# P.V of the first seven units in column tiles, with one Ln and one product for both heads

## The chip, the cores and the metric

The kernel runs on one core of one Trainium2 chip. The metric is device time in microseconds (us). A ratio is the mean time of one kernel's fast runs over that of the kernel before's fast runs in the same rounds, on the same chip, so it is not quite the ratio of the medians that are quoted beside it. The engines are TensorE (PE), ScalarE (ACT), VectorE (DVE), GpSimd (POOL, which issues most transfers here) and SyncE (SP).

## The reference

Attention with a relative position bias, then a layer with a squared ReLU. Cut to what matters:

```python
batch, n_heads, seq, head_dim = (8, 8, 576, 64)
scores = scale * np.matmul(q, k.transpose(0, 1, 3, 2)) + bias          # bias by distance, 32 buckets
attn = np.exp(scores - max)
attn = attn / (np.sum(attn, axis=-1, keepdims=True) + 1e-09)
x = np.matmul(attn, v)                                                  # "P.V"
h = np.maximum(x @ w_in, 0.0)                                           # 512 -> 2048
out = h * h @ w_out                                                     # 2048 -> 512
```

## The kernel before

A *unit* is two heads and 192 queries; there are 96. For each, TensorE makes the scores, ScalarE the exponentials, VectorE multiplies in the bias. P.V then gives the values and, from a column block of constants beside V, the sums. The weights of one head's key tile are 128 columns: 64 of V and 64 of constants. So one head takes one PSUM bank, values in one half of the partitions and sums in the other (the second head the other way round), and five matmuls:

```python
def pv_mm(e, jts):                       # e: which head of the two
    def f():
        if (n, e) not in pvt:
            pv_tile(n, e)                # one bank a head
        for jt in jts:                   # key tiles; jt 4 is the shared short one
            pv = pvt[n, e][:, 0:IC]      # 128 partitions x 192
            io(nc.tensor.matmul(
                pv if jt < 4 else pv.rearrange("p (g c) -> p g c", g=2),
                vz[:, jt, 2 * hp + e, :],                                  # 128 columns
                ets[n, jt // 2][:, e, ds(jt % 2 * IC, IC)] if jt < 4 else last_keys(n),
                start=(not mixed and jt == 0), stop=(jt == 3)))
```

The division is done as values x exp(-ln(sums)): one Ln a head, one Exp for both, one product a head:

```python
def ln(e):                                       # ScalarE, out of the sums' half of the bank
    ...
    nc.scalar.activation(out=rs[n][o : o + 64, :], in_=pvt[n, e][64 - o : 128 - o, 0:IC], func=LNF)
...
def mult(e):                                     # VectorE; a bank is free after its product
    ...
    nc.vector.tensor_tensor(out=x_sb[o : o + 64, hp, ds(ring(blk), IC)][:, ::-1],
                            in0=pvt[n, e][o : o + 64, 0:IC], in1=rs[n][o : o + 64, :], op=MULT)
```

The order on each engine is not written by hand. Every operation is recorded with estimated durations and its dependencies, and a list scheduler puts all of them in order when the kernel is built. One estimate: 0.095 us on TensorE when the row tiling changes. From unit 17 on another form of P.V is used, which this change does not touch.

The softmax here doesn't subtract the row's maximum and nothing guards it: scores larger than these inputs give would overflow.

Of the kernel before, what the change touches and what calls it, by code (L numbers as in the profile page):

```python
# [12 lines left out]
FP32 = mybir.dt.float32  # L13
FP16 = mybir.dt.float16
EXPF = mybir.ActivationFunctionType.Exp
LNF = mybir.ActivationFunctionType.Ln
RELUF = mybir.ActivationFunctionType.Relu
COPYF = mybir.ActivationFunctionType.Copy
MULT = mybir.AluOpType.mult
# [5 lines left out]
IC, NB = 192, 3  # L25
# [9 lines left out]
P, T0 = 4.07, 8.0  # L35


PV_BANKS, PV_MORE = [("p0", "p1"), ("f1", "f2")], 7


F1_LAG, F2_LAG = 4.8, 19.5
# [50 lines left out]
class Plan:  # L92
# [10 lines left out]
    def add(self, eng, stream, occ, lat, fn, deps=(), due=0.0, load=0.0, rows=128, more=False):  # L103
        o = Op(eng, occ, lat, fn, deps, due, load, rows, more)
        self.streams.setdefault(eng, {}).setdefault(stream, deque()).append(o)
        return o
# [78 lines left out]
def kernel(  # L185
# [10 lines left out]
    nc = tc.nc  # L196
    assert (_bucket(np.arange(128, S)) == NBK - 1).all()

    def io(ins):
        return tc.keep_in_program_order(ins)  # L200
# [15 lines left out]
    nr_pool = ctx.enter_context(tc.tile_pool(name="nr", bufs=2))  # L216
# [20 lines left out]
    x_sb = single.tile([128, 4, RING], FP16, name="x_sb")  # L237
# [9 lines left out]
    add = plan.add  # L247
# [81 lines left out]
    for out_, in_, t in (  # L329
# [9 lines left out]
            name=nc.get_next_instruction_name(),  # L339
# [123 lines left out]
    qts, kts, sts, ets, rs, pvt, hpt, rts, ypt, yts, tpt = ({} for _ in range(11))  # L463
# [3 lines left out]
    banks = {"f1": None, "f2": None, "p0": tv, "p1": warmed, "s0": None, "s1": None}  # L467
# [2 lines left out]
    plan.wait = lambda: 0.3 if units[0] < RUN_FROM else 0.02  # L470
    plan.fill = (lambda: units[0] == 0, 0.12, lambda: warm_up(1))
    s_last, kq_ready = {}, {}
    mults, ets_last, pv_ops = {}, {}, {}
    block_mults, f1_ops, f2_ops, sq_ops = {}, {}, {}, {}

    first_use = {4 * b + hp: n for n, (b, ic, hp) in reversed(list(enumerate(UNITS)))}
# [226 lines left out]
    def last_keys(n, rows=slice(None)):  # L703

        return ets[n, 0][rows, :, 2 * IC :]

    def values_need(n, e, jts=range(5)):

        b, ic, hp = UNITS[n]
        loads = [x for h_, x in zip([0, 0, 1, 1, 2, 3, 4, 5, 6, 7], loads_v[b]) if h_ in (e, 2 * hp + e)]  # L710
        return [o for g in {jt // 2 % 2 for jt in jts} for o in ets_last[n, g]] + loads

    def values_banks(o, n, es):


        def need(at):
            best = None
            for tags in [vbank[n]] if n in vbank else PV_BANKS if n < PV_MORE else PV_BANKS[:1]:
                x = [banks[tags[e]] for e in es]
                if not any(i.at is None for i in x if i):  # L720
                    t = max([at] + [i.done for i in x if i])
                    if best is None or t < best[0]:
                        best = t, tags
            return best

        def took(tags):
            vbank[n] = tags
            for e in es:
                banks[tags[e]] = mults[n][e]
            units[0] = n + 1  # L730

        o.need, o.took = need, took

    def pv_tile(n, e):
        tag = vbank[n][e]
        pvt[n, e] = (psF if tag[0] == "f" else psP).tile([128, 512], FP32, tag=tag, name=f"pv{e}")
        return pvt[n, e]
# [23 lines left out]
    def values(n, mixed=None):  # L761

        b, ic, hp = UNITS[n]
        vz = vzs[b % 2]
        pieces = ((0, 1), (2, 3)) if mixed else ((0, 1, 4), (2, 3))

        def pv_mm(e, jts):
            def f():
                if (n, e) not in pvt:
                    pv_tile(n, e)  # L770
                for jt in jts:
                    pv = pvt[n, e][:, 0:IC]
                    io(
                        nc.tensor.matmul(  # L774
                            pv if jt < 4 else pv.rearrange("p (g c) -> p g c", g=2),
                            vz[:, jt, 2 * hp + e, :],
                            ets[n, jt // 2][:, e, ds(jt % 2 * IC, IC)] if jt < 4 else last_keys(n),
                            start=(not mixed and jt == 0),
                            stop=(jt == 3),
                        )  # L780
                    )

            return f

        pv_ops[n] = []
        for e in range(2):
            for jts in pieces:
                o = add(
                    "PE",
                    "pv",  # L790
                    0.0825 * len(jts),
                    0.0825 * len(jts) + 0.22,
                    pv_mm(e, jts),
                    values_need(n, e, jts) + [mixed],
                    T0 + P * (n + 1.1 + 0.1 * e if mixed else n + 1.6 + 0.1 * e),
                )
                if not mixed and jts[0] == 0:
                    values_banks(o, n, (e,))
            pv_ops[n].append(o)

    def ring(blk):
        return blk * IC % RING

    def normalise(n):

        b, ic, hp = UNITS[n]
        blk = NB * b + ic
        mults[n] = []

        def ln(e):  # L810
            def f():
                if e == 0:
                    rs[n] = nr_pool.tile([128, IC], FP32, tag="r", name="r")
                o = 64 * e
                io(
                    nc.scalar.activation(  # L816
                        out=rs[n][o : o + 64, :], in_=pvt[n, e][64 - o : 128 - o, 0:IC], func=LNF
                    )
                )

            return f

        def mult(e):
            def f():
                o = 64 * e
                io(
                    nc.vector.tensor_tensor(  # L827
                        out=x_sb[o : o + 64, hp, ds(ring(blk), IC)][:, ::-1],
                        in0=pvt[n, e][o : o + 64, 0:IC],
                        in1=rs[n][o : o + 64, :],  # L830
                        op=MULT,
                    )
                )

            return f

        lns = [
            add("ACT", "ln", 0.31, 0.38, ln(e), [pv_ops[n][e]] + (mults[n - 2] if n > 1 else []), T0 + P * (n + 1.3))
            for e in range(2)
        ]  # L840
        x = add(
            "ACT",
            "ln",
            0.26,
            0.41,
            lambda: io(nc.scalar.activation(out=rs[n], in_=rs[n], func=EXPF, scale=-1.0)),  # L846
            lns,
            T0 + P * (n + 1.3),
        )
        free = f1_ops.get(blk - RING // IC, [])  # L850
        for e in range(2):
            mults[n].append(add("DVE", "mult", 0.29, 0.42, mult(e), [x] + free, T0 + P * (n + 1)))
        block_mults.setdefault(blk, []).extend(mults[n])


# [176 lines left out]
    for n in range(N + 1):  # L1032
        if RUN_FROM < n < N:
            mixed_in = []
            scores(n, lambda *x: mixed_in.append(values_mixed(n - 1, *x)))
            values(n - 1, *mixed_in)
        else:
            if n < N:
                scores(n)
            if n:  # L1040
                values(n - 1)
        if n:
            normalise(n - 1)
            for blks in GROUPS:
                if n - 1 == max(i for i, (b, ic, hp) in enumerate(UNITS) if NB * b + ic in blks):
                    layer1(blks)
                    layer2(blks)
        if n == N:
            break
        b, ic, hp = UNITS[n]  # L1050
        if last_use[4 * b + hp] == n:
            keys(4 * b + hp + KB)
        if b and (ic, hp) == (0, 0) and b < B - 1:

            loads_v[b + 1] = [x for i in range(8) for x in load_v(b + 1, i, pv_ops[n - 1])]
        if b and (ic, hp) == (1, 0) and b + 2 < B:
            halves[b + 2] = halve(b + 2)
# [32 lines left out]
```

## Time and profile before

| | before |
|---|---|
| time | 426.37 us, median of 3 (426.30 to 426.77); with later runs of the same build 426.34 |
| span of the profiled run | 422.2 us |
| busy, share of the span | PE 96%, DVE 74%, ACT 72% |

The span of a profile is some 1.8 us shorter than the time of the same run. In the first sixth the three engines wait for each other, so that is where fewer or shorter ScalarE and VectorE instructions can pay. The lines that show this, and what TensorE does later, stand in the prediction.

### The profile page before, as it was taken

The page shows a single profiled execution, that of the slowest core. Times are in us where ns is not written, and L with a number is a line of the kernel's source. Part 1 is how long each engine was busy: PE and PEld are TensorE (multiplying, and loading weights), DVE is VectorE, ACT ScalarE, POOL GpSimd, SP SyncE. Part 2 cuts the span into 40 slices and gives each one's busy share as a digit, 9 for nine tenths or more (in the row PEclk, how much of TensorE's full clock was granted, in tenths as well). Part 3 has the DMA queues.
Part 4 walks back from the last instruction along what each step waited for, and adds up shares of the span by engine and source line. Part 5 has one row for each costly group of instructions (what it writes and reads, how often), then busy time and mean ns, then how long its engine had stood idle before and what let it go on. Part 6 is the DMA issues. An engine that isn't in the chain of part 4 may idle for free.

```text
span 422.2 us, 9448 instructions
## 1 busy us (share of the span) xinstructions
PE 406.7 (96%) x3631; PEld 262.0 (62%) x3631; DVE 313.5 (74%) x940; ACT 302.9 (72%) x588; POOL 130.7 (31%) x176
## 2 busy tenths in 40 slices
PE   7888989899999999999999999999999999999996
PEld 4666876466685666666666566666666666665554
DVE  6889687668785777777776878777777877778762
ACT  5898796797897887787778777887787777770000
POOL 7956649409400491008600391006000000000000
PEclk8899999999999999999999999999999999999999
DMA  9999999969965699159925599169004110001012
GB/s 136 152 200 149 176 135 77 149 119 83 123 66 99 92 102 93 54 103 92 127 35 87 96 100 105 47 92 107 26 22 69 49 50 2 26 26 51 25 51 75
DMA packets 164765, 36.61 MB, mean 87 GB/s; under 512 B 152584, under 2 KB 160064, under 8 KB 164720
## 3 DMA queue, kind: packets, MB, share of 16 engines
q0 software_dynamic: 129728, 19.11, 59.1%
q1 hardware_dynamic: 34896, 16.90, 16.4%
q8 instruction: 28, 0.46, 0.5%
q14 instruction: 17, 0.14, 0.1%
q10 hardware_dynamic: 96, 0.00, 0.0%
HBM read 37.56 MB, written 16.52 MB: 128 GB/s over the span
## 4 chain that ended last, share of the span: by engine, by line
PE 85%; DVE 9%; ACT 3%; issue 1%; DMA 1%; DVEq 0%
PE yps L985 29%; PE hps L902 27%; PE pv L774 15%; PE st L640 7%; PE pv L748 3%; PE st L615 2%; DVE y L998 2%; DVE et L684 2%; ACT et L666 2%; DVE x_sb L827 1%; DVE rt L921 1%; DVE g_sb L917 1%; DMA raw_k<-in_k_dram 1%; PE tp L502 1%; ACT r L816 1%
## 5 line engine op out<-in xcount | busy, mean ns | idle before, releaser
L666 ACT ACTIVATE et<-st 128x960 f16<-128x960 f32 x192 | 167.9, 883 | 55.0 <-PE st L640 54.1
L902 PE MATMUL hps<-x_sb,w_in_sb 128*128 128x384 f16 (+1 forms) x896 | 152.0, 303 | 1.1 <-DVE rt L921 0.6
L985 PE MATMUL yps<-w_out_sb,g_sb 128*128 128x512 f16 (+1 forms) x592 | 148.6, 373 | 2.6 <-DVE y L998 1.7
L902 PEld LDWEIGHTS <-w_in_sb 128*128 128x128 f16 x896 | 83.3, 98 | 49.8 <-issue 2.1
L684 DVE TENSOR_TENSOR et<-et,tb_sb 128x384 f16<-128x384 f16 (+2 forms) x288 | 78.2, 310 | 33.3 <-ACT et L666 29.6
L251 POOL DMA_DIRECT2D vz<-in_v_dram x80 | 57.8, 743 | 129.4 <-PE pv L774 72.6
L985 PEld LDWEIGHTS <-g_sb 128*128 128x128 f16 x592 | 57.2, 98 | 51.1 <-issue 6.0
L774 PE MATMUL pv<-et,vz 128*128 128x192 f16 x804 | 84.9, 247 | 2.8 <-DVE x_sb L827 1.6
L827 DVE TENSOR_TENSOR x_sb<-pv,r 64x192 f16<-64x192 f32 x192 | 67.8, 353 | 21.6 <-ACT r L846 18.3
L917 DVE TENSOR_TENSOR g_sb<-rt 128x384 f16<-128x384 f16 x192 | 68.0, 358 | 7.5 <-ACT rt L913 2.5
L774 PEld LDWEIGHTS <-vz 128*128 128x128 f16 x804 | 62.4, 98 | 18.0 <-issue 15.2
L816 ACT ACTIVATE r<-pv 64x192 f32<-64x192 f32 x192 | 62.6, 326 | 7.7 <-PE pv L774 2.8
L913 ACT ACTIVATE rt<-hps 128x384 f16<-128x384 f32 x96 | 46.7, 487 | 28.6 <-PE hps L902 28.4
L921 DVE TENSOR_SCALAR rt<-hps 128x384 f16<-128x384 f32 x96 | 53.5, 557 | 13.4 <-PE hps L902 10.3
L640 PE MATMUL st<-qt,kt 64*128 64x192 f16 x768 | 50.2, 246 | 0.6 <-ACT et L666 0.6
L251 POOL DMA_DIRECT2D k<-in_k_dram x48 | 31.0, 684 | 27.4 <-DMA q<-in_q_dram 16.2
L846 ACT ACTIVATE r<-r 128x192 f32<-128x192 f32 x96 | 35.0, 364 | 3.1
L640 PEld LDWEIGHTS <-kt 64*128 64x128 f16 x768 | 31.9, 95 | 3.5 <-issue 1.5
L998 DVE TENSOR_SCALAR y<-yps 128x512 f32<-128x512 f32 (+1 forms) x37 | 25.0, 676 | 7.6 <-PE yps L985 6.8
L615 PEld LDWEIGHTS <-km_sb 128*128 128x128 f16 x192 | 18.2, 99 | 17.4 <-issue 3.0
L615 PE MATMUL st<-qt,km_sb 128*128 128x96 f16 x192 | 24.2, 208 | 0.7 <-ACT et L666 0.5
L251 POOL DMA_DIRECT2D q<-in_q_dram x18 | 24.6, 1401 | 0.0
(33 smaller groups left out, 117.1 us busy)
## 6 DMA issues: line engine op xcount, KB each, us to landing
out_dram<-y SPq DMA_DIRECT2D x35, 256.0 KB, 2.5
vz<-in_v_dram POOLq DMA_DIRECT2D x64, 64.0 KB, 3.1
q<-in_q_dram POOLq DMA_DIRECT2D x18, 192.0 KB, 8.2
k<-in_k_dram POOLq DMA_DIRECT2D x48, 72.0 KB, 7.0
w_in_sb<-in_moe_w_in_dram POOLq DMA_DIRECT2D x4, 512.0 KB, 9.5
w_out_sb<-in_moe_w_out_dram POOLq DMA_DIRECT2D x4, 512.0 KB, 9.8
qh<-in_q_dram POOLq DMA_DIRECT2D x8, 144.0 KB, 6.4
kh<-in_k_dram POOLq DMA_DIRECT2D x7, 144.0 KB, 7.2
```

Source lines behind the costliest of these rows:

```text
L251: return lambda: io(eng.dma_start(out=out_, in_=in_))
L615: nc.tensor.matmul(st[:, g, 2 * IC : 2 * IC + IC // 2], km_sb[:, p % KB, :], qts[p][:, ds(c0 + g * IC // 2, IC // 2)], start=True, stop=True,)
L640: nc.tensor.matmul(st[:, e, ds(i * IC, IC)], kts[p][rows, ts(2 * g + i, 128)], qts[p][rows, ds(c0, IC)], start=True, stop=True,)
L666: io(nc.scalar.activation(out=et, in_=sts[n, g][:, :, 0:w], func=EXPF, scale=SCALE))
L684: nc.vector.tensor_tensor(out=sl, in0=sl, in1=tb_sb[:, 2 * hp : 2 * hp + 2, ds(w0, w)], op=MULT)
L774: nc.tensor.matmul(pv if jt < 4 else pv.rearrange("p (g c) -> p g c", g=2), vz[:, jt, 2 * hp + e, :], ets[n, jt // 2][:, e, ds(jt % 2 * IC ...
L816: nc.scalar.activation(out=rs[n][o : o + 64, :], in_=pvt[n, e][64 - o : 128 - o, 0:IC], func=LNF)
L827: nc.vector.tensor_tensor(out=x_sb[o : o + 64, hp, ds(ring(blk), IC)][:, ::-1], in0=pvt[n, e][o : o + 64, 0:IC], in1=rs[n][o : o + 64, :], ...
L902: nc.tensor.matmul(hps[:, ds(i * w, w)], w_in_sb[:, kk, ts(nt, 128)], x_sb[:, kk, ds(o, w)], start=(kk == 0), stop=(kk == 3),)
L917: io(nc.vector.tensor_tensor(out=g_sb[:, ts(u, k), o : o + w], in0=rt, in1=rt, op=MULT))
L921: io(nc.vector.tensor_scalar_max(out=rt, in0=hpt[blks, u][:, 0 : 2 * IC], scalar1=0.0))
L985: nc.tensor.matmul(ypt[j], g_sb[:, nt, ds(128 * m % RING, 128)], w_out_sb[:, nt, cols], start=(nt == 0), stop=(nt == 15),)
```

## The change

Its intent: put the values of both heads into one bank and the sums of both into another. Each 128-column matmul then becomes two of 64 columns; the two heads' matmuls go to different column halves of the array, where they can run at the same time. One Ln over 128 partitions then serves both heads, and so does one product. Only the first seven units get this form (`COLS`).

```diff
+COLS = 7
...
+        def columns(jts):
+            def f():
...
+                for jt in jts:
+                    for u in range(2):           # 0: values, 1: sums; one bank each
+                        for e in range(2):       # head e in partitions 64 e and up
+                            pv = pvt[n, u][64 * e : 64 * e + 64, 0:IC]
+                            io(nc.tensor.matmul(
...
+                                    vz[:, jt, 2 * hp + e, ds(64 * (u ^ e), 64)],
...
+        def ln_both():
+            io(nc.scalar.activation(out=rs[n], in_=pvt[n, 1][:, 0:IC], func=LNF))
+
+        def mult_both():
+            io(nc.vector.tensor_tensor(
+                    out=x_sb[:, hp, ds(ring(blk), IC)][:, ::-1], in0=pvt[n, 0][:, 0:IC], in1=rs[n], op=MULT))
...
-                banks[tags[e]] = mults[n][e]
+                banks[tags[e]] = mults[n][e] if n >= COLS or e == 0 else lns[n]
```

The cuts leave out the recording of these operations with the scheduler (P.V of a unit in two pieces of 12 and 8 matmuls, Ln and product of 0.31 and 0.29 us) and line breaks.

More of the change, by code (lines that the diff above doesn't have):

```diff
@@ L472 @@
     s_last, kq_ready = {}, {}
-    mults, ets_last, pv_ops = {}, {}, {}
+    mults, lns, ets_last, pv_ops = {}, {}, {}, {}
     block_mults, f1_ops, f2_ops, sq_ops = {}, {}, {}, {}
@@ L785, in values @@
         pv_ops[n] = []
+        def columns(jts):
+            def f():
+                if (n, 0) not in pvt:
+                    for u in range(2):
+                        pv_tile(n, u)
+                for jt in jts:
+                    for u in range(2):
+                        for e in range(2):
+                            pv = pvt[n, u][64 * e : 64 * e + 64, 0:IC]
+                            io(
+                                nc.tensor.matmul(
+                                    pv if jt < 4 else pv.rearrange("p (g c) -> p g c", g=2),
+                                    vz[:, jt, 2 * hp + e, ds(64 * (u ^ e), 64)],
+                                    ets[n, jt // 2][:, e, ds(jt % 2 * IC, IC)] if jt < 4 else last_keys(n),
+                                    start=(jt == 0),
+                                    stop=(jt == 3),
+                                )
+                            )
+            return f
+        if n < COLS:
+            for jts in pieces:
+                o = add(
+                    "PE",
+                    "pv",
+                    0.165 * len(jts) + 0.1,
+                    0.165 * len(jts) + 0.32,
+                    columns(jts),
+                    values_need(n, 0, jts) + values_need(n, 1, jts),
+                    T0 + P * (n + 1.6),
+                )
+                if jts[0] == 0:
+                    values_banks(o, n, (0, 1))
+            pv_ops[n].append(o)
+            return
         for e in range(2):
@@ L808, in normalise @@
         mults[n] = []
+        def ln_both():
+            rs[n] = nr_pool.tile([128, IC], FP32, tag="r", name="r")
+            io(nc.scalar.activation(out=rs[n], in_=pvt[n, 1][:, 0:IC], func=LNF))
+        def mult_both():
+            io(
+                nc.vector.tensor_tensor(
+                    out=x_sb[:, hp, ds(ring(blk), IC)][:, ::-1], in0=pvt[n, 0][:, 0:IC], in1=rs[n], op=MULT
+                )
+            )
         def ln(e):
@@ L835, in mult @@
             return f
-        lns = [
-            add("ACT", "ln", 0.31, 0.38, ln(e), [pv_ops[n][e]] + (mults[n - 2] if n > 1 else []), T0 + P * (n + 1.3))
-            for e in range(2)
-        ]
+        war = mults[n - 2] if n > 1 else []
+        if n < COLS:
+            x = [lns.setdefault(n, add("ACT", "ln", 0.31, 0.38, ln_both, pv_ops[n] + war, T0 + P * (n + 1.3)))]
+        else:
+            x = [
+                add("ACT", "ln", 0.31, 0.38, ln(e), [pv_ops[n][e]] + war, T0 + P * (n + 1.3)) for e in range(2)
+            ]
         x = add(
@@ L846, in normalise @@
             lambda: io(nc.scalar.activation(out=rs[n], in_=rs[n], func=EXPF, scale=-1.0)),
-            lns,
+            x,
             T0 + P * (n + 1.3),
@@ L850, in normalise @@
         free = f1_ops.get(blk - RING // IC, [])
-        for e in range(2):
-            mults[n].append(add("DVE", "mult", 0.29, 0.42, mult(e), [x] + free, T0 + P * (n + 1)))
+        for f in [mult_both] if n < COLS else [mult(e) for e in range(2)]:
+            mults[n].append(add("DVE", "mult", 0.29, 0.42, f, [x] + free, T0 + P * (n + 1)))
         block_mults.setdefault(blk, []).extend(mults[n])
```

## The prediction

> **What bounds the kernel now.** I read the page first, then windows, then the chain and the timeline of the part that the change touches. Columns of the windows view: stretch, its length, then busy us of PE, PE's weight load, DVE, ACT and POOL with instruction counts, clock, DMA share, GB/s.
>
> ```profile
> span 422.2 us, 9448 instructions
> PE 406.7 (96%) x3631; PEld 262.0 (62%) x3631; DVE 313.5 (74%) x940; ACT 302.9 (72%) x588; POOL 130.7 (31%) x176
> ...
> PE   7888989899999999999999999999999999999996
> ```
>
> Each digit is a tenth of busy time in one fortieth (10.6 us) of the span. From about 60 us on TensorE (PE) is full, so there the end moves by PE's own work alone. The first sixth is different, and all seven units of the change (a unit: two heads, 192 queries) lie in it:
>
> ```profile
> 15.30:24.00 8.70, 7.20 (x101) 5.80 (x100) 8.27 (x30) 8.29 (x20) 7.34 (x11) 1.00 1.39 198
> 24.00:34.00 10.00, 8.24 (x105) 5.84 (x105) 8.34 (x29) 9.76 (x19) 6.78 (x10) 1.00 1.28 203
> 34.00:44.00 10.00, 8.36 (x120) 7.26 (x120) 9.37 (x29) 8.61 (x18) 6.60 (x10) 1.00 1.42 128
> 44.00:51.20 7.20, 7.20 (x85) 6.70 (x82) 4.36 (x14) 5.10 (x11) 5.53 (x6) 1.00 1.17 187
> ```
>
> The first three rows are 28.7 us. ScalarE (ACT) is busy 8.29 + 9.76 + 8.61 = 26.7 us of them (93%), VectorE (DVE) 26.0 us (91%). PE is less full than its digits say, because a matmul's busy time includes its latency. From the single matmuls' starts (start to next start, less columns/2.4 GHz) I get 10.4 us in which the array streams nothing. The fourth row is a block of 80 layer-1 matmuls in one go: PE works off a backlog there.
>
> Who holds PE in 15 to 44 us (us in total, times, longest), and what the chain is made of there (start, length, what):
>
> ```profile
> PE pv L774 <- DVE x_sb L827: 1.6, 3, 0.7
> PE tp L502 <- DVE kt L519: 1.1, 1, 1.1
> ```
>
> ```profile
> 23.77 0.33 ACT r L816
> 24.10 0.02 issue
> 24.12 0.33 ACT r L816
> ...
> 26.42 0.33 ACT r L816
> 26.75 0.02 issue
> 26.78 0.33 ACT r L816
> 27.11 0.02 issue
> 27.13 0.37 ACT r L846
> 27.50 0.02 issue
> 27.53 0.35 DVE x_sb L827
> 27.88 0.03 issue
> 27.91 0.36 DVE x_sb L827
> ```
>
> So the pairs of Ln (L816) and of products (L827) stand on the chain one behind the other, once per head. P.V waits for a PSUM bank until a product has read it. This is what the change goes for.
>
> **What the Trainium skill says.** (1) "TensorEngine Tiling (Array Packing)", Key Properties: column tiles run loads and matmuls independently, and changing the mode drains TensorE. The trace before already has the form: the transposes (L502) write 64 columns each, one head above the other. Their view gives 203/206/230 ns for one, and the timeline shows twelve in 0.45 us. One after the other at 96 columns / 2.4 GHz = 40 ns, they would need 11 x 40 + 206 = 646 ns; in pairs, 5 x 40 + 206 = 406 ns. The single starts show pairs 2 to 28 ns apart and about 41 ns from pair to pair.
>
> ```profile
> 20.66 0.45 PE L502 MATMUL tp<-id_sb,qh 96*64 96x96 f16 x12 [1.06 <-DVE kt L519]
> ...
> 22.83 1.00 PE L774 MATMUL pv<-et,vz 128*128 128x192 f16 x10
> ```
>
> The drain is there too: between matmuls of different tile shape I find 95 to 99 ns more than the streaming time (full to 64-row tiles, 102 times, median 98; back, 96 times, median 95; column to full at least 98). (2) The same page, Restrictions: column tiling turns Fast Weight Load off. The 64-column loads of the transposes take 106 to 110 ns against 98 for 128 columns, but two of them fit in each 41 ns step, so in 80 ns steps they should not bind. (3) "ScalarE: Activation LUTs": one element per cycle and lane, so partitions are free. The trace agrees: Ln of 64x192 takes 326 ns, Exp of 128x192 364 ns. (4) "PSUM — Partial Sum Buffer", the four PSUM rules: a first matmul clears bank x quadrants, so two heads may share a bank in different halves; the transposes share one already, though without accumulating.
>
> **The change part by part.**
> - *Ln.* Units 0 to 6 lose one each: 7 x 0.326 = 2.28 us of ACT. The remaining one has 128 partitions and 192 columns still: about 0.33 us.
> - *Product.* Likewise 7 x 0.353 = 2.47 us of DVE.
> - *Matmuls.* 70 become 140 of 64 columns. Paired, a key tile takes 2 x 82 ns as before (ten matmuls now: 9 x 82 + 246 = 0.98 us; the line says 1.00). Array time: unchanged, 7 x 0.82 us.
> - *Mode switches.* The built orders, counted by tile shape from the first P.V on: 230 switches before, 246 after; up to the end of the 80-matmul block, 32 and 47. So 16 x 0.096 = 1.5 us more PE time, nearly all of it in the part with 10.4 us idle (3.1 us of which, 32 x 0.096, are switches now).
> - *Order.* The order is set at build time by the kernel's list scheduler. In the new one all P.V of unit 6 comes before the first layer-1 matmul (before: after the first eight of them). Up to the ACT work on the 80-block, two more K/Q copies go to ACT (2 x 0.48 us) and one fewer to DVE. Net: ACT 2.28 - 0.97 = 1.3 us less, DVE 2.47 + 0.48 = about 3 us less.
> - *Banks.* The bank of the sums is free after the Ln instead of after the second product. The first head's Ln now waits for all ten key-tile passes of the unit, but the second's did so already.
>
> The chain before shows three second Lns or second products in the lines above (24.12, 26.78, 27.91), plus products at 17.34 and 18.87 that may be one of a pair. I estimate 1.4 to 2.0 us off the chain, between ACT's 1.3 and DVE's 3. Against that, about half of the 15 switches (1.44 us) fall where PE is on the chain: 0.4 to 0.7 us back. Net, the 80-block should start 0.8 to 1.6 us earlier; I take 1.2.
>
> Does that reach the end? After the block PE is nearly full, and 44 to 70 us show few PE waits for DMA (0.2 us). The weights the block needs are there in time:
>
> ```profile
> L251 POOL DMA_DIRECT2D w_in_sb<-in_moe_w_in_dram x4: 747/787/854, 17.2 to 27.0; - x4
> ...
> DMA to landing us min/median/max: 7.5/9.5/11.0
> ```
>
> The last is issued at 27.0 and lands at most 11.0 us later, by 38, against a block start of 44. So 1.2 us early should stay 1.2 us early. The later order differs in few places (layer-1 and layer-2 groups swap here and there), worth perhaps 0.5 us either way.
>
> Sum: 426.37 - 1.2 = 425.2 us.
>
> **Rivals.**
> 1. *The column tiles do not overlap.* The transposes share one moving operand, P.V's two heads stream different ones. Serial, each unit costs 0.82 us more, 5.7 us in all; with some of the idle time taking it up, +2 to +4 us: 428 to 430. Against: the transposes' pairs are separate instructions and overlap. One chance in twelve.
> 2. *The switches eat the gain.* If all 1.5 us fall on the chain and ACT yields only 1.3, the time is 426.2 to 426.6. For: both numbers are of one size, and P.V is on the chain. Against: 7.3 us of real PE waits in that part.
> 3. *The full relief arrives.* DVE is the engine on most links of the chain between 31 and 44 us; if its 3 us come off and banks come free earlier, the time is 423.5 to 424.
> 4. *A DMA takes the place of the waits.* DMA is busy without a break here, but the last w_in is six us early; I give it little.
>
> **Range and chances.** Rivals 2 and 3 set the range: 423.8 to 427.0. Runs of before spread by 0.5 us. Two per cent is 8.5 us, more than everything removed (2.28 + 2.47), so faster by 2% is nearly out; slower by 2% would need more than rival 1. Within 2%: 0.98.
>
> **What would show it.** In the profile after: seven Lns and products of 128x192 at about 0.33 and 0.35 us; P.V of one unit, twenty matmuls, in about 1.0 us (1.8 would be rival 1); PE's gap at a change of shape still near 96 ns; the 80-block starting near 42.8 us instead of 43.95 (43.9 or later would be rival 2, before 42 rival 3); the same lead at the end. I am wrong if the lead at the block is lost later, or if ACT and DVE, relieved, just wait for PE or for each other.

## The result, and the profile after

| | before | after |
|---|---|---|
| time, median | 426.34 us (4 runs, 425.79 to 426.77) | 424.64 us (4 runs, 424.53 to 424.82) |
| ratio | | 0.9961, 95% interval 0.9944 to 0.9979 |
| span of the profiled run | 422.2 us | 423.1 us |
| first P.V matmul, profiled run | 15.29 us | 16.48 us |
| block of 80 layer-1 matmuls starts, profiled run | 43.95 us | 45.11 us |

The time fell by 1.7 us, within 2% and inside the range. But the profiled run of after is longer than that of before, and its early marks are later. This is no contradiction: the profiled run of before took 424.02 us, 2.3 us less than its median. One profile each cannot carry a difference of 1.7 us. The experiments therefore start with both kernels again.

The page of after, in the lines that answer to those of before:

```profile
span 423.1 us, 9579 instructions
...
PE 409.5 (97%) x3701; PEld 262.6 (62%) x3701; DVE 309.3 (73%) x928; ACT 301.9 (71%) x586; POOL 130.7 (31%) x176
...
PE   7999899899999999999999999999999999999996
```

VectorE is busy 4.2 us less, ScalarE 1.0 us less. TensorE's 2.8 us more mean little: two profiles of before differ by 2.2 us in it (406.7 and, in e1, 408.9). The stretches of the prediction, same columns as there:

```profile
15.30:24.00 8.70, 8.23 (x155) 6.34 (x154) 6.62 (x24) 6.96 (x15) 7.36 (x12) 1.00 1.42 202
24.00:34.00 10.00, 9.22 (x128) 6.74 (x124) 6.56 (x22) 9.24 (x20) 6.26 (x9) 1.00 1.27 204
34.00:44.00 10.00, 8.35 (x121) 5.60 (x120) 9.62 (x29) 9.71 (x18) 7.17 (x9) 1.00 1.42 129
44.00:51.20 7.20, 6.50 (x75) 6.17 (x75) 4.71 (x14) 3.62 (x9) 4.76 (x6) 1.00 1.18 188
```

Up to 34 us VectorE has become slack (13.2 us busy of 18.7, before 16.6). From 34 to 44 us it is as full as before (9.62 against 9.37): part of its work has moved there. What TensorE waits for between 15 and 44 us (us in total, times, longest):

```profile
PE tp L504 <- ACT kt L519: 0.5, 1, 0.5
PE pv L776 <- DVE x_sb L877: 0.4, 1, 0.4
```

P.V's wait for a product's bank is down from 1.6 to 0.4 us, and the 1.1 us of the transposes for a copy became 0.5. The fused instructions, by shape (count, busy us, mean ns), and the P.V of the first three units in the timeline (start, length; the first line is two units):

```profile
L855 DVE TENSOR_TENSOR x_sb<-pv,r 128x192 f16<-128x192 f32 x7 | 2.5, 358 | 1.3 <-ACT r L899 1.2
L851 ACT ACTIVATE r<-pv 128x192 f32<-128x192 f32 x7 | 2.3, 332 | 1.7 <-PE pv L799 1.5
```

```profile
16.48 2.04 PE L799 MATMUL pv<-et,vz 128*64 128x192 f16 x40
...
18.91 1.02 PE L799 MATMUL pv<-et,vz 128*64 128x192 f16 x20
```

Twice the partitions cost next to nothing: 332 ns for 326, 358 for 353. Twenty matmuls of a unit take 1.02 us, where ten of double width took 1.00. The column tiles do overlap.

### The profile page after: what moved, and what is told of

Same layout as the page of the kernel before. It is cut to its first block, busy times and chain, and to the rows that moved or that the text cites. A ratio compares the mean times of both kernels' runs of the same rounds, so it can differ in the third digit from the quotient of the medians.

```text
span 423.1 us, 9579 instructions
## 1 busy us (share of the span) xinstructions
PE 409.5 (97%) x3701; PEld 262.6 (62%) x3701; DVE 309.3 (73%) x928; ACT 301.9 (71%) x586; POOL 130.7 (31%) x176
## 3 DMA queue, kind: packets, MB, share of 16 engines
q1 hardware_dynamic: 34896, 16.90, 16.6%
## 4 chain that ended last, share of the span: by engine, by line
PE 83%; DVE 7%; DMA 4%; ACT 2%; POOL 2%; issue 1%; DVEq 0%; POOLq 0%
PE yps L1038 29%; PE hps L955 28%; PE pv L776 14%; PE st L642 6%; PE pv L750 3%; PE st L617 2%; DVE y L1051 2%; DMA kh<-in_k_dram 2%; DMA w_in_sb<-in_moe_w_in_dram 1%; DVE x_sb L877 1%; DVE rt L974 1%; DVE et L686 1%; DMA raw_k<-in_k_dram 1%; DVE g_sb L970 1%; POOL vz L253 1%
## 5 line engine op out<-in xcount | busy, mean ns | idle before, releaser
L776 PE MATMUL pv<-et,vz 128*128 128x192 f16 x734 | 77.6, 247 | 2.2 <-DVE qt L521 1.6
L877 DVE TENSOR_TENSOR x_sb<-pv,r 64x192 f16<-64x192 f32 x178 | 62.8, 353 | 22.6 <-ACT r L899 19.7
L966 ACT ACTIVATE rt<-hps 128x384 f16<-128x384 f32 x98 | 47.8, 487 | 31.4 <-PE hps L955 30.4
L776 PEld LDWEIGHTS <-vz 128*128 128x128 f16 x734 | 56.5, 98 | 16.9 <-issue 14.7
L866 ACT ACTIVATE r<-pv 64x192 f32<-64x192 f32 x178 | 57.9, 325 | 7.1 <-PE pv L776 2.7
L974 DVE TENSOR_SCALAR rt<-hps 128x384 f16<-128x384 f32 x94 | 52.4, 557 | 13.4 <-PE hps L955 10.4
L642 PE MATMUL st<-qt,kt 64*128 64x192 f16 x768 | 51.6, 248 | 0.3 <-ACT et L668 0.3
```

Source lines behind the costliest of these rows:

```text
L642: nc.tensor.matmul(st[:, e, ds(i * IC, IC)], kts[p][rows, ts(2 * g + i, 128)], qts[p][rows, ds(c0, IC)], start=True, stop=True,)
L776: nc.tensor.matmul(pv if jt < 4 else pv.rearrange("p (g c) -> p g c", g=2), vz[:, jt, 2 * hp + e, :], ets[n, jt // 2][:, e, ds(jt % 2 * IC ...
L974: io(nc.vector.tensor_scalar_max(out=rt, in0=hpt[blks, u][:, 0 : 2 * IC], scalar1=0.0))
```

## The experiments

Each kernel ran in five rounds beside the kernel before. The first eight ran on one chip, e9 to e11 on another and e12 on a third, so their times are compared through the ratios. "Order kept" means that the sequence of instructions on every engine was checked to be that of the kernel named, apart from the edit.

**e1 and e2: both kernels once more.** No edit.

> The kernel before, unchanged, against itself. It sets the noise: ratio 1.000 within 0.001 and 426.3 us. Its profile gives a second look at the start: in the first profile of before the first P.V matmul started at 15.29 us and the block of 80 layer-1 matmuls at 43.95 us, in the one of after at 16.48 and 45.11. If the 1.2 us at the start belong to the run and not to the kernel, this profile may show a start anywhere between 15 and 17 us.

> The changed kernel, unchanged. The difference of 1.7 us should come again: ratio 0.996, about 424.6 us. In the profile, the theory of the prediction (lead won early and kept) wants the time from the first P.V matmul to the 80-block about 1.2 us shorter than before's 28.66; the rival (lead lost again before the block, gain from elsewhere) wants it within 0.3 us of that, as in the first profile of after (28.63).

Measured: before 426.24 us (ratio to itself 1.0004, 0.9985 to 1.0023); after 424.52 us (ratio 0.9979, 0.9955 to 1.0002). The sign and size come again, 1.6 us by the medians, though this interval alone just reaches 1. The spread within one kernel is the surprise: before took 424.07 to 426.93 us, after 422.83 to 425.94 us, where the prediction had reckoned with 0.5 us from three runs.

The marks of the profiles show where spread and gain lie. They are times of TensorE matmul starts in the trace; the block is that of the 80 layer-1 matmuls.

| profile | first P.V at | first P.V to block | block to end of span |
|---|---|---|---|
| before | 15.29 | 28.66 | 378.30 |
| before again (e1) | 16.83 | 29.41 | 378.19 |
| after | 16.48 | 28.62 | 377.95 |
| after again (e2) | 15.42 | 27.67 | 377.96 |

The last column hardly moves between two profiles of one kernel (0.1 us). So what is won or lost before the block reaches the end, and what comes after the block is 0.3 us shorter in after. The middle column moves by 0.8 to 1.0 us between runs of one kernel; its means differ by 0.9 us (29.04 against 28.15). That agrees with the prediction's 1.2 but, with two profiles each, does not establish it. In e1 the granted TensorE clock was 0.50 from 23.4 to 26.8 us, which may be part of its 29.41; in after, too, the first 0.4 us ran at half clock. The two profiles with a full clock all the way from the first P.V to the block, before and e2, differ by 1.0 us (28.66 and 27.67).

The first column moves by 1.5 us in one and the same kernel. Two things go with a late first P.V. One is the load of the identity table for the first transposes:

```profile
PE tp L502 <- DMA id_sb<-c_id: 0.4, 1, 0.4
```

```profile
PE tp L502 <- DMA id_sb<-c_id: 1.2, 1, 1.2
```

The first line is TensorE's wait in the profile of before, the second in that of e1, the same kernel.

The other is the clock, and here the windows view misleads. It reads 1.00 also where the trace holds no clock record, and seven of the fourteen profiles have no record before 15.8 to 19.7 us. The score matmuls (192 columns) tell the clock without it: in the fourteen profiles one took 336 to 365 ns under a record of 0.50 and 239 to 254 under one of 1.00. First a window of after's profile that reads 1.00 (the clock is the third number from the end); then the score matmuls from 9 to 14 us, in after and in e7 (below), a build with the same work before its first P.V (count, ns at least, in the middle, at most):

```profile
10.00:15.00 5.00, 5.00 (x68) 3.22 (x65) 3.72 (x12) 3.92 (x7) 4.82 (x7) 1.00 0.75 107
```

```profile
L642 PE MATMUL st<-qt,kt x16: 337/364/364, 9.8 to 12.8; 64*128 64x192 f16 x16
```

```profile
L642 PE MATMUL st<-qt,kt x24: 239/243/253, 9.2 to 13.4; 64*128 64x192 f16 x24
```

So after's TensorE ran at half clock there. Between 9 and 14 us it did so in twelve of the fourteen profiles, and their first P.V came at 15.29 to 17.80 us. In the two others, e7 and e9, it came first of all, at 14.62 and 14.48 us, though their identity tables landed later than that of before (5.27 and 5.17 us against 4.63). Among the twelve, a later table on the whole goes with a later first P.V. No run separates the two.

**e3: the instructions put back, order kept.**

```diff
-            io(nc.scalar.activation(out=rs[n], in_=pvt[n, 1][:, 0:IC], func=LNF))
+            for o in (0, 64):
+                io(nc.scalar.activation(out=rs[n][o : o + 64, :], in_=pvt[n, 1][o : o + 64, 0:IC], func=LNF))
...
-            io(nc.vector.tensor_tensor(out=x_sb[:, hp, ...], in0=pvt[n, 0][:, 0:IC], in1=rs[n], op=MULT))
+            for o in (0, 64):
+                io(nc.vector.tensor_tensor(out=x_sb[o : o + 64, hp, ...], in0=pvt[n, 0][o : o + 64, 0:IC], ...))
```

> The changed kernel with each of its seven Lns and seven products issued as two of 64 partitions again, everything else and the order on every engine the same. This puts 2.3 us back on ScalarE and 2.5 us back on VectorE and nothing on TensorE. If the removed instructions are what wins (the prediction), 1.2 to 1.7 us come back: ratio to before 0.999 to 1.000. If the order of the schedule wins, the time stays near 424.6 us, ratio 0.996 to 0.997.

Measured: 429.24 us, ratio 1.0072 (1.0051 to 1.0094). Putting back the seven Lns and seven products costs 4.7 us against e2, far more than I expected, and about as much as their own lengths together: 7 x 0.33 + 7 x 0.35 = 4.8 us. The profile shows the instructions, fourteen of each at the old length, and VectorE waiting for ScalarE in front of them:

```profile
L857 DVE TENSOR_TENSOR x_sb<-pv,r 64x192 f16<-64x192 f32 x14 | 5.0, 355 | 4.0 <-ACT r L904 3.8
L852 ACT ACTIVATE r<-pv 64x192 f32<-64x192 f32 x14 | 4.5, 323 | 2.6 <-PE pv L799 2.5
```

From first P.V to block it took 31.99 us instead of 28.62 and 27.67, 3.8 us over their mean; the rest of this profile's excess lies before the first P.V (17.80 us). In this fixed order the chain runs P.V, Ln, Exp, product, next P.V. The chain of e3 up to the block has all seven added Lns on it, but only two of the seven added products:

```profile
19.65 0.32 ACT r L852
19.99 0.34 ACT r L852
...
23.76 0.35 DVE x_sb L857
24.12 0.36 DVE x_sb L857
```

That is 7 x 0.33 + 2 x 0.36 = 3.0 of the 3.8 us. The first 1.9 us after its first P.V also ran at half clock. So 4.7 us may be somewhat too high a price, and that it equals the sum of the lengths is in part chance.

**e4: the new order with the old instructions.** The sequence is that of after; in the places of the fused operations stand before's ten 128-column matmuls, two Lns and two products, one bank a head (cut).

```diff
-                for jt in jts:
-                    for u in range(2):
-                        for e in range(2):
-                            pv = pvt[n, u][64 * e : 64 * e + 64, 0:IC]
+                for e in range(2):
+                    for jt in jts:
+                        pv = pvt[n, e][:, 0:IC]
```

> The order of the changed kernel on every engine, but with before's instructions in it: 128-column matmuls of one head after the other, two Lns and two products a unit, one bank a head. It has before's work (no new mode switches) in after's order. If the order alone wins: 424.6 us or less, ratio 0.995 to 0.997. If the instructions win: 426 us or more, since this order was made for shorter chains: ratio 0.999 to 1.003.

Measured: 430.42 us, ratio 1.0112 (1.0085 to 1.0140). The order by itself wins nothing: with before's instructions it loses 4.3 us against before. The expectation was wrong in one point: this order has new mode switches, 43 up to the block in its trace against before's 32, which is 11 x 0.096 = 1.1 us of TensorE. The rest I put down to an order made for shorter operations; no run isolates it.

**e5 and e6: Lns alone, products alone.** Either half of the edit of e3.

> The changed kernel with only its seven Lns issued as two of 64 partitions again, order kept: 2.3 us back on ScalarE alone. Splitting both cost 4.7 us (429.24 against 424.52). If the chain of the first seven units runs through ScalarE and VectorE in turn, so that each removed instruction counts about its own length, this alone costs 2.0 to 2.8 us: 426.5 to 427.3 us. If ScalarE alone is the bound there, it costs nearly all of the 4.7 us; if VectorE alone is, under 0.7 us.

> The changed kernel with only its seven products issued as two of 64 partitions again, order kept: 2.5 us back on VectorE alone. In turn: 1.7 to 2.6 us, 426.2 to 427.1 us, and the sum with the run that splits the Lns is near 4.7 us. VectorE was idle for 5.6 of the 18.7 us between 15.3 and 34 us of the changed kernel's first profile, so if ScalarE is the bound this costs under 1 us.

Measured: 427.44 us (ratio 1.0039, 1.0015 to 1.0063) with the Lns split, 427.28 us (1.0030, 1.0010 to 1.0050) with the products split: 2.9 and 2.8 us over e2, each a little over my ranges. From first P.V to block they took 30.37 and 30.34 us, against a mean of 28.15 of the two profiles of after: 2.2 us each, close to the 2.3 and 2.5 us put back. So neither engine alone is the bound of this stretch: the pieces stand in one chain and add. The chain of e5 has all seven added Lns on it; that of e6 has four of the seven added products, 1.4 us, and e6 ran at half clock for the first 3.5 us after its first P.V, so that its 2.2 us are not the products' alone. That the times differ by 0.6 us more than this stretch goes with a late first P.V (17.73 and 17.69 us), which these profiles have and which the edit, lying later, does not explain. Their identity table landed late: TensorE waited 2.1 us for it in e5 and 1.9 in e6.

```profile
PE tp L504 <- DMA id_sb<-c_id: 2.1, 1, 2.1
```

**e9: the layout alone, planned for it.** The column tiles and the two banks stay, but each unit keeps two Lns and two products, and the scheduler knows it.

```diff
-                banks[tags[e]] = mults[n][e] if n >= COLS or e == 0 else lns[n]
+                banks[tags[e]] = mults[n][e] if n >= COLS else lns[n] if e else mults[n][1]
...
-                        out=rs[n][o : o + 64, :], in_=pvt[n, e][64 - o : 128 - o, 0:IC], func=LNF
+                        out=rs[n][o : o + 64, :],
+                        in_=pvt[n, 1][o : o + 64, 0:IC] if n < COLS else pvt[n, e][64 - o : 128 - o, 0:IC],
...
-                        in0=pvt[n, e][o : o + 64, 0:IC],
+                        in0=pvt[n, 0 if n < COLS else e][o : o + 64, 0:IC],
```

> The column tiles and the two banks (values of both heads, sums of both heads) alone: the first seven units keep two Lns and two products, and the order is planned for them. Its P.V, banks and matmul work are the change's, its ScalarE and VectorE work is before's. If the removed instructions are the gain and the layout is neutral or a small cost, 426 to 427.5 us, ratio 1.000 to 1.003. If the banks that come free earlier and the larger pieces of P.V are half of the gain, about 425.5 us. It is below the run that splits both in an order made for the fused form (429.24) in either case, by what that order's misfit costs.

Measured: 425.71 us, with before at 425.65 us in these rounds: ratio 1.0003 (0.9978 to 1.0029). The layout alone is worth nothing that these runs resolve, neither as a gain from banks nor as a cost. By itself this does not prove that the gain is gone, as the interval overlaps that of e2 (0.9955 to 1.0002) and touches that of after's first rounds (0.9944 to 0.9979). P.V waits for the products again:

```profile
PE pv L799 <- DVE x_sb L868: 1.8, 2, 1.4
```

e3 and e9 have the same instructions. They differ in order alone, and by 0.7% in ratio (1.0072 against 1.0003), some 2.9 us. This is the part of e3's 4.7 us that is not the price of the instructions but of an order made for shorter ones. Switches are a good part of it: up to the block the trace of e9 has 29, that of e3 47 like after, 18 x 0.096 = 1.7 us of TensorE. So it is the planned order, and not the column tiles as such, that brings after's 15 more switches than before.

**e7 and e8: the same form for twelve and for seventeen units.** `COLS = 12`, `COLS = 17`, planned anew.

> The same change for the first twelve units: five more Lns (1.65 us) and five more products (1.77 us) removed, from the part between 31 and 56 us where VectorE is on most links of the chain. If a removed pair is worth there what it is worth in the first seven units (4.7/7 = 0.67 us), 3.3 us less than the changed kernel: 421.2 us. If the lead is swallowed in that part (by the weights' arrival at 38 us and the copies of keys and queries), within 0.7 us of 424.5. It is planned anew, so the order moves too.

> The same change for all seventeen units before the row-tiled form begins. The last five lie in 52 to 75 us, where TensorE is nearly full. Removed vector work should be worth nothing there and each unit adds about two mode switches of 0.096 us, 1 us in all: 0.5 to 1.5 us slower than the run with twelve. If the waits of that part (TensorE idle some 1.5 us beyond switches) shrink instead, up to 1 us faster than twelve.

Measured: twelve units 423.49 us (ratio 0.9938, 0.9907 to 0.9968), seventeen 424.18 us (0.9952, 0.9930 to 0.9974). Both are faster than before; between themselves and against after the intervals overlap, so the medians' 1.0 us from seven units to twelve is likely but not settled. It is less than a third of what the fixed-order price of 0.67 us a unit would give (3.3 us). In the profiles, from the first P.V to the end of the span, after took 406.57 and 405.63 us, twelve units 404.12, seventeen 403.67.

**e10 and e11: the mode switches made known to the scheduler.** Each P.V and transpose in column tiles is marked as another tile shape, so that the 0.095 us is counted; with seven and with twelve units.

```diff
                     values_need(n, 0, jts) + values_need(n, 1, jts),
                     T0 + P * (n + 1.6),
+                    rows=32,
```

> The changed kernel, with the scheduler told that the column-tiled operations (P.V of the first seven units, the transposes) differ in mode from the others, so that it counts 0.095 us for each switch as it does for the row tiles. The built order has 215 switches from the first P.V on, the changed kernel 228: 13 x 0.096 = 1.2 us less TensorE time. If a switch costs on the path what it takes (the prediction put half of them there), 0.6 to 1.2 us faster than 424.5; if the early part is bound by ScalarE and VectorE alone, no difference beyond 0.4 us.

> Both of the above with the fused form for twelve units: 213 switches against 224 of the run with twelve. If the gains add: 423.5 - 0.5 to 1.0 = 422.5 to 423.0 us, the best of all kernels here. If the order that the scheduler makes is luck, it may land anywhere from 422.5 to 425.

Measured: 425.01 us (ratio 0.9991, 0.9967 to 1.0015) and 423.61 us (0.9962, 0.9938 to 0.9986). Neither gains anything that can be seen against e2 (0.9979) and e7 (0.9938). Thirteen fewer switches, 1.2 us of TensorE by 0.096 us each, did not shorten the run. But the marks show where it went. From first P.V to block, e10 took 27.16 us against after's 28.62 and 27.67, and e11 26.29 against e7's 27.11: 1.0 and 0.8 us less, with 12 and 11 fewer switches there (35 and 36 against 47). From block to end they took 379.12 and 378.49 us, against 377.95 and 377.01: 1.2 and 1.5 us more. These builds also have another order before the first P.V and after the block, and each has one profile, so this is no clean test of a switch's price. It agrees with a switch costing about its length before the block, and says that the count over the whole program is no good guide to the time.

**e12: twelve units, and the identity table in one transfer with the one-hot table.**

```diff
-    small_in.append(small(oh_sb, oh_d.ap(), 2.8))
-    id_in = small(id_sb, id_d.ap(), 2.8)
+    id_in = small(const_sb, const_d.ap(), 2.8)     # 96 x 704: both tables
+    small_in.append(id_in)
```

> The run with twelve units, and besides the identity table of the first transposes loaded in one transfer with the one-hot table (issued second on its queue at about 1.2 us instead of third at 1.7 us); the order on every engine is the same. In the profiles so far the identity landed between 4.6 and 6.3 us, the one-hot table in front of it between 4.0 and 4.4 us, and a late identity went with a late first P.V (14.5 to 17.8 us). If that wait sets the start and is carried to the end: the table lands by 4.6 us, the first P.V starts at 14.5 to 15.5 us, and the time is 421.5 to 423.0 us with a smaller spread than 420.5 to 425.3. If the start's spread has another cause (the clock, the bias table's way through memory), the time stays near 423.5 us with the same spread.

Measured: 422.35 us (421.04 to 422.92), ratio 0.9911 (0.9894 to 0.9928). This is faster than before, and its interval lies below those of after (0.9944 to 0.9979, and e2's 0.9955 to 1.0002). Against e7 the intervals overlap. The spread of its six runs is 1.9 us, e7's was 4.8; but the kernel before, with its table untouched, also spread less on this chip (1.8 us against 2.9), so this is not shown to be the table's doing. The table landed at 4.53 us, as expected, and TensorE waited for it

```profile
PE tp L507 <- DMA const_sb<-c_both: 0.3, 1, 0.3
```

but the first P.V came at 15.80 us, later than I expected and later than e7's 14.62. In this profile the granted TensorE clock was 0.50 from 10 to 15 us; in e7's it was 1.00 there. So an early table does not by itself make an early start, and whether it helps at all is not shown: a half clock at the start goes with the lateness here too.

## Why the prediction was right

The time fell within the range, at 424.64 us for 425.2 predicted, and the fixed-order runs support the stated reason. By its steps:

- *Ln and product.* Right in count and length (332 and 358 ns), and the reason for the gain: with the removals undone in a fixed order (e3, e5, e6) it turns into a loss, with intervals clear of after's; with the layout but without these removals (e9) no gain is left to see, though there the intervals overlap.
- *Matmuls in pairs.* Right: 1.02 us a unit, and 82 or 83 ns from pair to pair (192 columns), close to the 2.4 GHz that the prediction reckons with. The first rival, tiles that do not overlap, is refuted by the same line.
- *Mode switches.* Their number up to the block is right (the trace has 32 and 47). But the total was misstated: 230 and 246 are about the counts over the whole program (230 and 247 in the traces); from the first P.V on they are 211 and 228. The trace also has the switch at 92 to 98 ns at its shortest for the column tiles. That half of their time falls on the path is not shown by any run; e10 and e11, which were 1.0 and 0.8 us shorter before the block with 12 and 11 fewer switches, point rather to nearly all of it.
- *What comes off the chain.* "1.4 to 2.0 us" was a term without a fixed size. With the order held it is 4.7 us (e2 against e3), 3.8 of them between first P.V and block; against a build planned for the old instructions it is about 1.0 us (ratio 0.9979 against e9's 1.0003, on another chip and with overlapping intervals). The prediction read single links of one chain and could not see that the scheduler makes good most of a longer chain by other orders. In the two profiles with a full clock from the first P.V to the block, TensorE's array is empty for 10.4 us (before) and 9.4 us (e2). (e1's 11.2 counts streaming at half clock as emptiness.) Taking off the switches (32 and 47 times 0.096 us, 3.1 and 4.5 us), the real waits fell from 7.3 to 4.9 us: 2.4 us won, 1.4 us handed back. By this account both of the prediction's terms were too small (1.4 to 2.0 and 0.4 to 0.7 us), and that its net of 1.2 came so near to 1.0 is partly luck.
- *The lead reaches the end.* Right: the time from the block to the end is the same to 0.1 us in both profiles of each kernel, and in e3, e5 and e6, which have after's order, it is 377.92 to 377.94 us as well. It moves by 0.3 us for the new order ("perhaps 0.5 us either way").
- *The sign to look for.* "The 80-block starting near 42.8 us" was a bad one. It came at 45.11 and 43.09 us in two profiles of the same build, because the first P.V starts anywhere between 14.5 and 17.8 us in the fourteen profiles. Marks have to be taken from the first P.V.
- *Rivals.* By its sign at the first profile, a block at 43.9 us or later, I would have believed the second rival (the switches eat the gain). The medians speak against it. The third (423.5 to 424 us) was not reached with seven units.

One early mark shows how an intermediate lead can mislead. The product of the seventh unit ended 19.3 and 20.1 us after the first P.V in the profiles of before, and 13.9 us in both of after. Of those 5.4 us or more, about 0.9 us are left at the block: the new order does the copies of keys and queries later, and VectorE, with 5.5 us idle from 15.3 to 34 us, has them to do afterwards.

What stays open: how much of the gain lies before the block and how much at its start, which two profiles each cannot tell; whether twelve or seventeen units is better; and what moves the start, where clock and table have not been separated.

## What to carry to other kernels

When a scheduler orders the instructions, an instruction taken out in its fixed order and one taken out with a new plan have different worths (here 4.7 and about 1.0 us), so test a part of a change both ways. Putting two half-filled results side by side, so that one vector instruction reads all 128 partitions, costs TensorE no streaming time where its column tiles run in pairs. Before comparing two traces of a 0.4% change, look at how far two traces of one kernel differ, and take marks from the first common event, not from zero. Where the clock may have changed, look at the length of one kind of matmul: a clock that reads 1.00 can be one that was not recorded.

## What the Trainium skill lacked or had wrong

- "TensorEngine Tiling (Array Packing)", Key Properties: it says that a change of tiling mode drains TensorE, without a size. Here a switch between full, 64-row and 64-column tiles takes 92 to 98 ns over the streaming time at its shortest, nearly the same whichever way.
- The same page, Restrictions: column tiling turns Fast Weight Load off. The page gives no size for it. Here 64-column loads take 112 ns in the profile against 98 for full ones of twice the columns, and twenty matmuls of 192 columns still run in 1.02 us, so they stay hidden at that length.
- "TensorE: Matmul & The Clock Gate", Part 1: it tells of a half clock at the start and after idle windows, but not how busy TensorE must be for the full clock. Here, by records and lengths of matmuls, TensorE ran at half clock up to 14.3 to 21.2 us in twelve of the fourteen profiles (five of them had 3.4 us at full clock before), although the view has TensorE busy (latency included) for 4.79 to 5.00 of the 5 us from 10 to 15.
- No page that was read has how much the landing of a small early load varies: the identity table of 36 KB, third on its queue, landed between 4.63 and 6.33 us in thirteen profiles.
